# Gates of two more chunks spread by TensorE, one store of all gates, clearing divided among engines, and unread matmuls at the start

## The chip, the cores and the metric

One core of a Trainium2 chip runs the whole program: TensorE (PE), VectorE (DVE), ScalarE (ACT), GpSimd (POOL) and SyncE (SP), which issues nearly all DMAs here. Each engine works off its own list of instructions in order; between engines, semaphores order the work. The metric is the device time of one launch in microseconds. The kernel before takes 523.4 us, the median of three runs (523.13 to 523.64).

## The reference

Three layers follow each other: an mLSTM attention over 2 sequences of 768 steps with 8 heads of width 40, a mixture of 8 experts with the two best per token, and a dense layer with x cos(x) in its middle. Only the first one matters for the change:

```python
for t in range(S):
    m_new = np.maximum(f_gate[:, :, t] + m, i_gate[:, :, t])
    f_stab = np.exp(f_gate[:, :, t] + m - m_new)
    i_stab = np.exp(i_gate[:, :, t] - m_new)
    m = m_new
    C = f_stab * C + i_stab * np.einsum('bhd,bhe->bhde', vt, kt)
    n = f_stab * n + i_stab * kt
    h_tilde = np.einsum('bhde,bhe->bhd', C, qt)
    y[:, :, t] = sigmoid(o_gate) * h_tilde / max(abs(n . qt), 1)
```

## The kernel before, in words

The steps of time are cut into 6 chunks of 128 for each of 2 sequences, 12 chunk steps in all. Within a chunk the recurrence becomes matmuls: scores of queries and keys (`mm_s`, line 247), weights made of the gates (`mk_w`, line 209, and a triangular select on POOL, line 210), their product (`mk_p`, line 256), the output from the product and from the state of the chunk before (`mm_out`, lines 306 and 310), and the new state (`mm_state`, line 266; `mk_state`; `mk_decay`).

The gates lie with the 16 pairs of sequence and head on partitions and time along the free axis. `gates_a` runs the recurrences for a range of chunks on DVE (lines 90 to 97: a scan, two elementwise operations, a clamp, a running sum for each chunk); `gates_b` (lines 108 to 110) makes two further rows from them; `gates_t` transposes the gates on TensorE (line 121), and `gates_c` copies the results to `tok`, `tokG` and `kdec`. The weights need the running sum of a head along time on all 128 partitions. There are two ways to this. For chunks 0 and 1, `mm_g` (line 196) spreads it by TensorE, eight transposes of a column of `tokG` into two PSUM banks, from which ScalarE reads. For all others, `gates_a` stores the sums to DRAM (`GD`, line 102), and `load_gb` (line 175) reads them back with the partition axis repeated, 512 KB for each chunk. There are two stores: chunks 0 to 3, and chunks 4 and 5. `mk_w` and `mk_e` (lines 223 and 226) read either the PSUM banks (`pg`) or the loaded tile (`gb`).

The order of each engine's list is the order of the calls in the program. Ahead of the loop, lines 808 to 837 call the loads, the gates of chunks 0 to 3, and the scores, weights and product of chunks 0 and 1. In the loop, step n (`att_step`) makes the output of chunk n, the scores and weights of chunk n + 2 and the product of chunk n + 1, and issues loads ahead (`loads`). SP's list holds these loads, the stores of the gates and those of the outputs, in order. PSUM tiles come from rotating pools: `psA` of four banks, `psS` of three, `psM` of one. A new tile waits until all readers of the tile that had its bank are done. `psS` serves `mm_g`, `mm_state` and `mm_out`; `psM` serves the transposes of the gates and of the outputs (`rt_a`, `rt_b`).

Clearing: the tiles for queries and keys have unused rows that have to be zero, as have those for `kb` and the state. POOL clears them (lines 137, 141, 145), DVE half of one (line 136).

Of the kernel before, what the change touches and what calls it, by code (L numbers as in the profile page):

```python
# [9 lines left out]
FT = mybir.dt.float32  # L10
FR = mybir.dt.float32r
BF = mybir.dt.bfloat16
I32 = mybir.dt.int32
U32 = mybir.dt.uint32
AF = mybir.ActivationFunctionType
# [3 lines left out]
B, H, S, D = 2, 8, 768, 40  # L19
NH = H // 2  # L20
C = 128
# [19 lines left out]
def tile_mlstm_moe_moe2(ctx, tc, qk, kv, og, gi, gf, wcat, noise, wm1, wm2, cst, out):  # L41
# [15 lines left out]
    def psS():  # L57
        return ps.tile([128, 512], FT, name="pS", tag="S", bufs=3)

    def psM():  # L60
        return ps.tile([128, 512], FT, name="pM", tag="M", bufs=1)
# [7 lines left out]
    ident = cp.tile([128, 128], FT, name="ident")  # L69
    cc_ = cp.tile([128, 341], FT, name="cc")  # L70
    A.preload_act_table_set("exp_and_others")

    g_r = cp.tile([16, C], FT, name="g_r")
    V.memset(g_r, 1.0)
    V.memset(g_r[:, 0:1], 0.0)
    V.memset(g_s, 0.0)
    tok = cp.tile([128, NC, 16], FT, name="tok")
    tokG = cp.tile([128, 2, 16], FT, name="tokG")
    kdec = cp.tile([128, NC, 16], FT, name="kdec")
    GD = dr.tile([NC, 16, C], FT, name="gd")  # L80

# [2 lines left out]
    def gates_a(c0, c1):  # L84
        a, z = c0 * C, c1 * C
        s = slice(a, z)
        a1 = max(a, 1)
        if a == 0:
            V.memset(g_g[:, 0:1], 0.0)
        V.tensor_tensor_scan(out=g_m[:, s], data0=g_f[:, s], data1=g_i[:, s],  # L90
                             initial=(-1e30 if a == 0 else g_m[:, a - 1:a]), op0=OP.add, op1=OP.max)
        V.tensor_tensor(out=g_g[:, a1:z], in0=g_f[:, a1:z], in1=g_m[:, a1 - 1:z - 1], op=OP.add)
        V.tensor_tensor(out=g_g[:, a1:z], in0=g_g[:, a1:z], in1=g_m[:, a1:z], op=OP.subtract)
        V.tensor_scalar(g_g[:, a1:z], g_g[:, a1:z], -110.0, None, op0=OP.max)
        for c in range(c0, c1):
            V.tensor_tensor_scan(out=g_G[:, c * C:(c + 1) * C], data0=g_r, data1=g_g[:, c * C:(c + 1) * C],
                                 initial=0.0, op0=OP.mult, op1=OP.add)
        if c0 < 2:
            A.activation(gG[:, s], g_G[:, s], AF.Copy)
        if c0 >= 2:  # L100
            d0 = 0 if c0 == 2 else c0
            Y.dma_start(GD[d0:c1].rearrange("c p t -> p c t"),
                        g_G[:, d0 * C:c1 * C].rearrange("p (c t) -> p c t", t=C))

    def gates_b(c0, c1):
        n = c1 - c0
# [16 lines left out]
    def gates_c(c0, c1):  # L123
        pv = PT[c0]
        V.tensor_copy(tok[:, c0:c1, :], pv[:, :, 0:16])
        if c0 < 2:
            V.tensor_copy(tokG[:, c0:c1, :], pv[:, :, 64:80])
        A.activation(kdec[:, c0:c1, :], pv[:, :, 32:48], AF.Exp)


    NB = 3
    QKS, KBS, STS = [], [], []
    for i in range(NB):
        t = ap_.tile([128, 4, NH, C], FT, name=f"qk{i}")
        if i == 1:
            V.memset(t[:, 0:2], 0.0)
        G.memset(t[:, 2 * (i == 1):], 0.0)
        QKS.append(t)
    for i in range(2):
        t = ap_.tile([128, H, 64], FT, name=f"kb{i}")  # L140
        G.memset(t, 0.0)
        KBS.append(t)
    for i in range(2):
        t = ap_.tile([128, NH, 82], FT, name=f"st{i}")
        G.memset(t, 0.0)
        STS.append(t)
    XD = dr.tile([B * S, KW], FT, name="xd")
    KO = H * D
# [12 lines left out]
    def load_qk(n):  # L161
        if n >= 2 * NC:
            return
        b, c = divmod(n, NC)
        d = L[n]
        t = d["qk"] = QKS[n % NB]
        Y.dma_start(t[0:D, 0:3], qk[b, c, 0])
        Y.dma_start(t[64:64 + D, 1:4], qk[b, c, 1])

    def load_gb(n):  # L170
        if n >= 2 * NC:
            return
        b, c = divmod(n, NC)
        t = L[n]["gb"] = ap_.tile([128, H, C], FT, name="gb", bufs=3)
        Y.dma_start(t, bass.AP(tensor=GD.tensor, offset=GD.offset + (c * 16 + b * H) * C,
                               ap=[[0, 128], [C, H], [1, C]]))
# [11 lines left out]
    def mm_g(n):  # L188
        b, c = divmod(n, NC)
        d = L[n]  # L190
        d["pg"] = []
        for u in range(2):
            p = psS()
            for w in range(4):
                h = b * H + 4 * u + w
                T.transpose(p[:, 128 * w:128 * w + 128], tokG[:, c, h:h + 1].to_broadcast([128, 128]), ident)
            d["pg"].append(p.rearrange("p (h t) -> p h t", t=C))

    def mk_w(n):
        if n >= 2 * NC:  # L200
            return
        b, c = divmod(n, NC)
        d = L[n]
        pg = [d["gb"][:, 0:4], d["gb"][:, 4:8]] if n >= 2 else d["pg"]
        w = d["w"] = ap_.tile([128, H, C], FT, name="wt", bufs=2)
        for u in range(2):
            for k in range(4):
                h = 4 * u + k
                A.activation(w[:, h, :], pg[u][:, k, :], AF.Exp, bias=tok[:, c, b * H + h:b * H + h + 1])
            G.affine_select(out=w[:, 4 * u:4 * u + 4, :], in_=w[:, 4 * u:4 * u + 4, :], pattern=[[0, 4], [1, C]],  # L210
                            compare_op=OP.is_ge, fill=0.0, base=0, channel_multiplier=-1)

    def mk_e(n):
        if n >= 2 * NC:
            return
        b, c = divmod(n, NC)
        d = L[n]
        if c:
            e = d["ge"] = ap_.tile([128, NH, C], FT, name="get", bufs=2)
            for s in range(2):  # L220
                r = slice(64 * s, 64 * s + 64)
                if n >= 2:
                    A.activation(e[r], d["gb"][r, s:H:2, :], AF.Exp)
                else:
                    for u in range(2):
                        A.activation(e[r, 2 * u:2 * u + 2, :], d["pg"][u][r, s:4:2, :], AF.Exp)
        if c < NC - 1:
            kb = d["kb"] = KBS[n % 2]
            G.tensor_tensor(out=kb[:, :, 0:D], in0=d["k"],
                            in1=kdec[:, c, b * H:b * H + H][:, :, None].to_broadcast([128, H, D]), op=OP.mult)  # L230
# [127 lines left out]


    tri = cp.tile([128, 128], BF, name="tri")  # L360
    ones = cp.tile([128, 128], BF, name="ones")
    io128 = cc_[:, 128:256]
    io32 = cc_[:, 256:288]
    tid = cc_[:, 288:300]
# [4 lines left out]
    def late_consts():  # L369
        Y.dma_start(cc_, cst[:, 128:469])  # L370
        Y.dma_start(wc, wcat)
        Y.dma_start(nz, noise)
# [433 lines left out]


    Y.dma_start(ident, cst[:, 0:128])
    load_qk(0)
    load_kv(0)  # L810
    load_qk(1)
# [11 lines left out]
    gates_b(1, 2)  # L823
    gates_t(1, 2)
    mm_s(0, (2, 3))
    gates_a(2, 4)
    gates_c(1, 2)
    mk_e(0)
    late_consts()
    load_gb(2)  # L830
    mk_p(0)
    mm_g(1)
    mk_w(1)
    mm_s(1)
# [3 lines left out]

    def loads(n):
        load_qk(n + 3)  # L840
        if n > 2 or n == 0:
            load_gb(n + 3)
        load_kv(n + 2)
        if n < 5:
            load_o(n + 1)
        if n == 2:
            load_gb(4)
            load_gb(5)

    def att_step(n):  # L850
        if n == 0:
            loads(0)
        if n:
            mk_e(n + 1)
        for f, a in pre.pop(n, []):
            f(*a)
        mm_state(n)
        if n:
            mm_s(n + 2, (0,))
        mm_out(n, (lambda w: mm_s(n + 2, (w + 1,))) if n else None)  # L860
        if n == 0:
            gates_t(2, 4)
        if n:
            rt_a(n - 1, psS if n == 7 else None)
        mm_s(n + 2, (3,) if n else range(NH))
        for f, a in mid.pop(n, []):
            f(*a)
        if n:
            rt_b(n - 1, psS if n == 9 else None)
        if n == 2:  # L870
            gates_t(4, NC)
        mk_state(n)
        mk_p(n + 1)
        mk_q(n + 1)
        mk_decay(n + 1)
        if n == 0:
            gates_c(2, 4)
        if n == 2:
            gates_c(4, NC)
        if n == 1:  # L880
            gates_a(4, NC)
        loads(n + 1)
        if n == 2 * NC - 1:
            mk_y(n)
        for f, a in fill.pop(n, []):
            f(*a)
        if n < 2 * NC - 1:
            mk_y(n)
        mk_w(n + 2)
        if n == 0:  # L890
            V.tensor_copy(tri, cc_[:, 0:128])
            V.tensor_copy(rb[:, 0], row0)
            V.memset(ones, 1.0)
            V.memset(os_[:, NC], 0.0)
        if n == 1:
            gates_b(4, NC)
        if n == 10:

            for p, r0, st, m in ((64, ROW0[2] + CAP2, 512, 6), (16, CAP1, 256, 2), (16, ROW1[0] + CAP1, 256, 2)):
                Y.dma_start(bass.AP(tensor=YD.tensor, offset=YD.offset + r0 * DM, ap=[[DM, p], [st * DM, m], [1, DM]]),  # L900
                            cc_[:p, None, 0:DM].to_broadcast([p, m, DM]))
# [128 lines left out]
    with tc.If(over > 0):  # L1030
        WD = [dr.tile([S, E], FT, name=f"wd{b}") for b in range(B)]
        for b in range(B):
            r = R[b]
# [125 lines left out]
```

## Time and profile before

| | |
|---|---|
| three timed runs | 523.64, 523.13, 523.40 us |
| profiled execution, its own time | 525.03 us |
| its span, first to last instruction | 523.3 us |
| PE busy | 490.2 us (94%) |
| DVE, ACT, POOL busy | 372.1, 325.7, 278.5 us |
| mean granted clock of TensorE | 0.992 |

Busy shares are means over the whole span. The attention steps are the first fifth of it; behind them the experts and the dense layer follow. A line of a timeline has the start, the time (of all instructions merged into it), engine, line, operation, what it writes and reads, and in brackets how long the engine was idle before it and what ended that. `x8` means eight instructions; a TensorE call on 32-bit data makes two or more of them. An engine's time on a line is not its occupation alone: neighbouring instructions overlap at their ends.

### The profile page before, as it was taken

What the parts mean: (1) busy time and instruction counts of PE and PEld (TensorE: products, weight loads), DVE (VectorE), ACT (ScalarE), POOL (GpSimd) and SP (SyncE); (2) the same over time, 40 slices, a digit from 0 to 9 for tenths busy, and PEclk for the clock granted to TensorE, in tenths of its full rate; (3) what the DMA queues carried; (4) which work ended last, traced back from release to release, by engine and by line L of the source; (5) the groups of instructions that cost most, each with busy time, mean ns of one, the idle gap of its engine ahead of it and who ended that gap; (6) DMA issues with size and microseconds to landing.
All of it is one profiled execution on the core that took longest, in us unless ns stands there. A gap on an engine that the chain in (4) does not pass through costs nothing.

```text
span 523.3 us, 9036 instructions
## 1 busy us (share of the span) xinstructions
PE 490.2 (94%) x3198; PEld 468.1 (89%) x3198; DVE 372.1 (71%) x791; ACT 325.7 (62%) x695; POOL 278.5 (53%) x246
## 2 busy tenths in 40 slices
PE   4799998999999999999999987999999999999994
PEld 3688887999899999999999976899999999999994
DVE  8774497678378777777775689688856665787772
ACT  3647867466465454545454655578787777777772
POOL 6445468665846867685857696274365347300000
PEclk9999999899999999999999999999999999999998
DMA  6789894695563828291929193030021003001001
GB/s 182 209 281 266 279 278 155 188 363 172 216 248 117 313 88 330 69 372 44 380 88 319 42 360 105 29 115 14 0 76 39 1 8 95 13 2 39 1 1 44
DMA packets 25909, 77.69 MB, mean 148 GB/s; under 512 B 3872, under 2 KB 11552, under 8 KB 25856
## 3 DMA queue, kind: packets, MB, share of 16 engines
q1 hardware_dynamic: 22752, 67.50, 37.2%
q0 software_dynamic: 3104, 9.54, 6.1%
q8 instruction: 27, 0.44, 0.3%
q14 instruction: 26, 0.21, 0.1%
HBM read 67.41 MB, written 9.62 MB: 147 GB/s over the span
## 4 chain that ended last, share of the span: by engine, by line
PE 69%; DVE 14%; DMA 7%; issue 4%; ACT 3%; POOL 2%; SPq 0%; DVEq 0%; POOLq 0%; ACTq 0%
PE pS L589 31%; PE pA L598 9%; PE pA L595 9%; PE pA L594 9%; DMA gb<-gd 2%; DMA xgt<-xd,idx 2%; PE pM L551 2%; PE pS L310 2%; PE pA L247 1%; PE pM L351 1%; PE pA L607 1%; PE pA L606 1%; POOL wl L582 1%; DVE xt L674 1%; DVE c_t L713 1%
## 5 line engine op out<-in xcount | busy, mean ns | idle before, releaser
L582 POOL TENSOR_TENSOR wl<-wraw,wh 128x704 fp32r<-128x704 f32 x69 | 122.9, 1787 | 59.9 <-ACT wh L580 56.3
L644 DVE SCALAR_TENSOR_TENSOR hb<-pS,hb 128x384 fp32r<-128x384 f32 (+2 forms) x128 | 45.9, 390 | 46.4 <-ACT hb L641 45.8
L580 ACT ACTIVATE wh<-wraw 128x704 fp32r<-128x704 f32 x80 | 62.8, 785 | 14.6 <-PE pA L606 8.2
L589 PE MATMUL pS<-xh,wh 128*128 128x448 f32 (+1 forms) x240 | 69.5, 344 | 0.4 <-ACT xh L553 0.4
L589 PE MATMUL pS<-xh,wl 128*128 128x448 f32 (+1 forms) x240 | 66.3, 330 | 0.9 <-POOL wl L582 0.9
L589 PE MATMUL pS<-xh,w 128*128 128x384 f32 x288 | 66.4, 339 | 0.5 <-DVE m_t L754 0.5
L594 PE MATMUL pA<-wh,hb 128*128 128x320 f32 x208 | 62.2, 309 | 0.0
L595 PE MATMUL pA<-wl,hb 128*128 128x320 f32 x208 | 62.2, 309 | 0.0
L739 ACT ACTIVATE m_t<-pS,magic 128x384 f32<-128x384 f32 x64 | 37.1, 579 | 30.4 <-PE pS L589 29.3
L641 ACT ACTIVATE hb<-pS 128x448 fp32r<-128x448 f32 (+1 forms) x80 | 37.6, 471 | 26.9 <-PE pS L589 20.0
L589 PEld LDWEIGHTS pS<-xh,w 128*128 128x128 f32 x288 | 50.0, 188 | 1.2 <-DVE m_t L754 1.1
L598 PE MATMUL pA<-wh,hb 128*128 128x320 f32 x208 | 44.3, 313 | 4.0 <-DVE hb L644 4.0
L754 DVE SCALAR_TENSOR_TENSOR m_t<-m_t,pS 128x384 f32<-128x384 f32 x64 | 35.4, 553 | 15.4 <-ACT m_t L753 15.1
L589 PEld LDWEIGHTS pS<-xh,wl 128*128 128x128 f32 x240 | 43.1, 190 | 3.3 <-POOL wl L582 1.1
L740 DVE TENSOR_SCALAR m_t<-m_t 128x384 f32<-128x384 f32 x64 | 23.3, 365 | 28.8 <-ACT m_t L739 28.6
L589 PEld LDWEIGHTS pS<-xh,wh 128*128 128x128 f32 x240 | 40.9, 190 | 1.4 <-ACT xh L553 0.6
L760 POOL TENSOR_TENSOR wl<-m_t,wh 128x384 fp32r<-128x384 f32 x25 | 25.4, 1017 | 31.0 <-ACT wh L758 21.7
L589 PE MATMUL pS<-xl,wh 128*128 128x448 f32 (+1 forms) x160 | 39.6, 329 | 0.0
L594 PEld LDWEIGHTS pA<-wh,hb 128*128 128x128 f32 x208 | 38.6, 186 | 0.6
L595 PEld LDWEIGHTS pA<-wl,hb 128*128 128x128 f32 x208 | 38.7, 186 | 0.6
L598 PEld LDWEIGHTS pA<-wh,hb 128*128 128x128 f32 x208 | 33.0, 186 | 6.0 <-DVE hb L644 5.9
L542 POOL DMA_INDIRECT xgt<-xd,idx x28 | 34.0, 1215 | 7.8 <-issue 3.4
(203 smaller groups left out, 1251.0 us busy)
## 6 DMA issues: line engine op xcount, KB each, us to landing
wraw<-wm SPq DMA_DIRECT2D x36, 704.0 KB
raw<-wm SPq DMA_DIRECT2D x16, 704.0 KB
qk<-qk SPq DMA_DIRECT2D x24, 240.0 KB
gb<-gd SPq DMA_DIRECT2D x10, 512.0 KB
kv<-kv SPq DMA_DIRECT2D x12, 324.0 KB
yd<-yt SPq DMA_DIRECT2D x22, 160.0 KB
wraw<-wm SPq DMA_DIRECT2D x8, 352.0 KB
xd<-xt SPq DMA_DIRECT2D x12, 192.0 KB
```

The source lines that it names most:

```text
L542: G.indirect_dma_start(out=t[:n, :], out_offset=None, in_=XD[0:S, :] if g < 2 else XD[:, :], in_offset=bass.IndirectOffsetOnAxis(ap=(idxe ...
L580: A.activation(wh, raw[:, f, :], AF.Copy)
L582: eng.tensor_tensor(out=wl, in0=raw[:, f, :], in1=wh.bitcast(FT), op=OP.subtract)
L589: T.matmul(p[:, :n], w[:, 128 * k:128 * k + 128], x[:, m, :], start=(i == 0), stop=(i == 7))
L594: T.matmul(a[:n, :DM], hh[:, s], wh[:, KW:], start=first, stop=False)
L595: T.matmul(a[:n, :DM], hh[:, s], wl[:, KW:], start=False, stop=False)
L598: T.matmul(a[:n, :DM], hl[:, s], wh[:, KW:], start=False, stop=last)
L641: A.activation(hh[:, :n], p[:, :n], AF.Relu)
L644: V.scalar_tensor_tensor(out=hb[:, o:o + z - a], in0=p[:, a:z], scalar=0.0, in1=hh[:, a:z].bitcast(FT), op0=OP.max, op1=OP.subtract)
L739: A.activation(t, m["p"], AF.Identity, bias=magic, scale=0.5 / PI)
L754: V.scalar_tensor_tensor(out=s, in0=s, scalar=1.0, in1=m["p"], op0=OP.subtract, op1=OP.mult)
L760: eng.tensor_tensor(out=m["hl"], in0=m["t"], in1=m["hh"].bitcast(FT), op=OP.subtract)
```

## The change

- `tokG` holds four chunks instead of two, and `gates_a` copies the sums of chunks 2 and 3 to the tile that is transposed (ScalarE, line 99), as it did for chunks 0 and 1. The chunks 2 and 3 are spread by `mm_g`, called in steps 0 and 1 for chunk n + 2, after the output's normalization is issued; the second half goes to the bank of `psM`. Their exponentials (`mk_g`, taken out of `mk_e`) follow their weights.
- The first store is gone, and so are the loads of chunks 2 and 3. One store of all six chunks is issued with `gates_a(4, 6)` in step 1.
- Ahead of the loop, `mk_p(0)` moves in front of `gates_a(2, 4)`, and both move behind `gates_c(1, 2)` and `mk_e(0)`.
- Clearing: POOL clears the first tile for queries and keys and half of the second; ScalarE clears the rest by copies of a zero column; DVE clears `kb` and the state tiles.
- The bf16 tile of ones is set at the start, and 14 matmuls of 128x384 on it are issued into a `psM` tile that nobody reads.

```diff
+    ones = cp.tile([128, 128], BF, name="ones")
+    V.memset(ones, 1.0)
...
-    tokG = cp.tile([128, 2, 16], FT, name="tokG")
+    tokG = cp.tile([128, 4, 16], FT, name="tokG")
...
-        if c0 < 2:
+        if c0 < 4:
             A.activation(gG[:, s], g_G[:, s], AF.Copy)
-        if c0 >= 2:
-            d0 = 0 if c0 == 2 else c0
-            Y.dma_start(GD[d0:c1].rearrange("c p t -> p c t"),
-                        g_G[:, d0 * C:c1 * C].rearrange("p (c t) -> p c t", t=C))
+        else:
+            Y.dma_start(GD.rearrange("c p t -> p c t"), g_G.rearrange("p (c t) -> p c t", t=C))
...
-        if c0 < 2:
+        if c0 < 4:
             V.tensor_copy(tokG[:, c0:c1, :], pv[:, :, 64:80])
...
+    zero = cp.tile([128, 1], FT, name="zero")
+    V.memset(zero, 0.0)
     for i in range(NB):
         t = ap_.tile([128, 4, NH, C], FT, name=f"qk{i}")
-        if i == 1:
-            V.memset(t[:, 0:2], 0.0)
-        G.memset(t[:, 2 * (i == 1):], 0.0)
+        if i == 0:
+            G.memset(t, 0.0)
+        else:
+            if i == 1:
+                G.memset(t[:, 0:2], 0.0)
+            for k in range(2 * (i == 1), 4, 2):
+                v = t[:, k:k + 2].rearrange("p a w t -> p (a w t)")
+                A.activation(v, zero.to_broadcast([128, 2 * NH * C]), AF.Copy)
...
-            p = psS()
+            p = psM() if u and n > 1 else psS()
...
+    def mk_g(n):
+        d = L[n]
+        e = d["ge"] = ap_.tile([128, NH, C], FT, name="get", bufs=2)
+        for s in range(2):
+            r = slice(64 * s, 64 * s + 64)
+            if n >= 4:
+                A.activation(e[r], d["gb"][r, s:H:2, :], AF.Exp)
+            else:
+                for u in range(2):
+                    A.activation(e[r, 2 * u:2 * u + 2, :], d["pg"][u][r, s:4:2, :], AF.Exp)
...
+    junk = psM()
+    for i in range(14):
+        T.matmul(junk[:, 0:384], ones, ones[:, None, :].to_broadcast([128, 3, 128]), start=True, stop=True)
...
     mm_s(0, (2, 3))
-    gates_a(2, 4)
     gates_c(1, 2)
     mk_e(0)
+    mk_p(0)
+    gates_a(2, 4)
     late_consts()
-    load_gb(2)
-    mk_p(0)
     mm_g(1)
     mk_w(1)
...
-        if n > 2 or n == 0:
+        if n > 2:
             load_gb(n + 3)
...
             mk_y(n)
+        if n < 2:
+            mm_g(n + 2)
         mk_w(n + 2)
+        if n < 2:
+            mk_g(n + 2)
```

## Rows read from the trace of the kernel before

**Rows 1.** Table by stretch: us, busy time of each engine, granted clock, DMA

```profile
135.00:320.00 185.00, 180.17 (x1111) 172.31 (x1110) 135.43 (x224) 98.84 (x175) 133.06 (x85) 1.00 0.59 218
```

**Rows 2.** Chain of waits, 0 to 62 us: start, us, what

```profile
29.41 4.29 DMA gd<-g_all
33.76 5.75 DMA gb<-gd
```

**Rows 3.** Timeline of ScalarE, 0 to 50 us

```profile
6.27 0.31 ACT L99 ACTIVATE g_all<-g_all 16x128 f32<-16x128 f32 x1 [4.17 <-DVE g_all L96]
...
9.02 2.17 ACT L209 ACTIVATE wt<-pS,tok 128x128 f32<-128x128 f32 x8 [0.93 <-PE pS L196]
...
15.00 2.17 ACT L209 ACTIVATE wt<-pS,tok 128x128 f32<-128x128 f32 x8 [0.47 <-PE pS L196]
17.01 1.32 ACT L226 ACTIVATE get<-pS 64x256 f32<-64x256 f32 x4
...
21.65 2.45 ACT L209 ACTIVATE wt<-gb,tok 128x128 f32<-128x128 f32 x8 [0.86 <-DMA gb<-gd]
...
39.60 2.44 ACT L209 ACTIVATE wt<-gb,tok 128x128 f32<-128x128 f32 x8 [1.05 <-DMA gb<-gd]
```

**Rows 4.** Timeline of TensorE, 7 to 71 us

```profile
11.77 1.99 PE L247 MATMUL pA<-qk 128*128 128x256 f32 x4
14.31 1.09 PE L196 MATMUL pS<-ident,tokG 128*128 128x128 f32 x8 [0.55 <-DVE tokG L127]
15.23 1.89 PE L247 MATMUL pA<-qk 128*128 128x256 f32 x8
...
18.11 2.01 PE L310 MATMUL pS<-kv,ppt 128*128 128x82 f32 x16 [0.27 <-ACT get L226]
...
21.87 0.88 PE L266 MATMUL pS<-kv,kb 128*104 128x82 f32 x8
24.76 0.67 PE L247 MATMUL pA<-qk 128*128 128x256 f32 x2 [2.02 <-DMA qk<-qk]
...
44.40 0.94 PE L351 MATMUL pM<-wc,xTt 128*128 128x128 f32 x6 [0.91 <-ACT xTt L344]
...
70.95 0.29 PE L440 MATMUL pM<-r_os,ones 128*128 128x48 bf16 x6
```

**Rows 5.** Timeline of SP's DMA issues, 14 to 18 us

```profile
14.13 0.34 SPq L102 DMA_DIRECT2D gd<-g_all  x1
...
17.78 0.32 SPq L167 DMA_DIRECT2D qk<-qk  x1
```

**Rows 6.** Timeline of DVE, 2 to 27 us

```profile
2.15 0.91 DVE L136 MEMSET qk<- 128x1024 f32 x1 [0.16 <-issue]
...
3.28 0.41 DVE L90 TENSOR_TENSOR_SCAN g_all<-g_all 16x128 f32<-16x128 f32 x1 [0.20 <-DMA g_all<-gi]
...
4.36 1.44 DVE L94 TENSOR_SCALAR g_all<-g_all 16x127 f32<-16x127 f32 x1
...
8.85 0.21 DVE L94 TENSOR_SCALAR g_all<-g_all 16x128 f32<-16x128 f32 x1
...
10.36 1.05 DVE L90 TENSOR_TENSOR_SCAN g_all<-g_all 16x256 f32<-16x256 f32 x1
...
13.38 0.73 DVE L96 TENSOR_TENSOR_SCAN g_all<-g_r,g_all 16x128 f32<-16x128 f32 x2
...
26.04 0.73 DVE L90 TENSOR_TENSOR_SCAN g_all<-g_all 16x256 f32<-16x256 f32 x1
```

**Rows 7.** Timeline of POOL, 5 us

```profile
5.20 1.06 POOL L141 MEMSET kb<- 128x512 f32 x2
```

**Rows 8.** Table by stretch around the first gather, columns as in rows 1

```profile
91.00:92.00 1.00, 0.55 (x3) 0.31 (x3) 0.00 (x0) 0.72 (x2) 1.00 (x3) 1.00 0.82 267
90.00:95.00 5.00, 3.53 (x17) 3.10 (x18) 1.94 (x6) 1.89 (x5) 4.55 (x6) 0.72 0.78 222
95.00:100.00 5.00, 5.00 (x42) 5.00 (x42) 4.80 (x13) 1.89 (x5) 2.88 (x3) 0.94 0.29 110
```

More of the change, by code (lines that the diff above doesn't have):

```diff
@@ L140, in tile_mlstm_moe_moe2 @@
         t = ap_.tile([128, H, 64], FT, name=f"kb{i}")
-        G.memset(t, 0.0)
+        V.memset(t, 0.0)
         KBS.append(t)
@@ L144, in tile_mlstm_moe_moe2 @@
         t = ap_.tile([128, NH, 82], FT, name=f"st{i}")
-        G.memset(t, 0.0)
+        V.memset(t, 0.0)
         STS.append(t)
@@ L203, in mk_w @@
         d = L[n]
-        pg = [d["gb"][:, 0:4], d["gb"][:, 4:8]] if n >= 2 else d["pg"]
+        pg = [d["gb"][:, 0:4], d["gb"][:, 4:8]] if n >= 4 else d["pg"]
         w = d["w"] = ap_.tile([128, H, C], FT, name="wt", bufs=2)
@@ L217, in mk_e @@
         d = L[n]
[L218 to L226, printed above, removed]
+        if c and n not in (2, 3):
+            mk_g(n)
         if c < NC - 1:
@@ L360, in tile_mlstm_moe_moe2 @@
     tri = cp.tile([128, 128], BF, name="tri")
-    ones = cp.tile([128, 128], BF, name="ones")
     io128 = cc_[:, 128:256]
@@ L892, in att_step @@
             V.tensor_copy(rb[:, 0], row0)
-            V.memset(ones, 1.0)
             V.memset(os_[:, NC], 0.0)
```

## The prediction

> **What bounds the kernel now.** I read the page's busy shares first, then a table by stretch, then the chain of waits, then the timelines of the single engines in the first 45 us. From 135 us on TensorE works 180.2 of 185 us [rows 1], so whatever the start gains or loses is still there at the end unless a wait takes it up on the way. All that the change touches lies before 45 us, and there TensorE does wait. The chain of waits [rows 2] runs, for the second chunk step, through the store of the gates of chunks 4 and 5 (29.41 us, 4.29 us until it has landed) and the load that reads it back, spread over all partitions (33.76, 5.75 us). ScalarE's weights of chunk 4 wait 1.05 us for that load and begin at 39.60 [rows 3], and TensorE waits 0.91 us at 44.40 for ScalarE work queued behind them [rows 4]. The other large hole is 2.02 us before 24.76 [rows 4], when the scores of chunk 3 wait for their queries and keys. That load goes out only at 17.78 [rows 5], because the spread load of chunk 2, ahead of it on SP, waits for the first store (14.13). Before that DVE sets the pace (the gate recurrences), and TensorE is at its lower level, 1.2 GHz: four score matmuls take 1.99 us at 11.77, eight take 1.89 us at 15.23 [rows 4], though the granted-clock column says 1.00 there too.
>
> **The change, part by part.** The sum is made on the profiled execution, span 523.3 us in a run of 525.03; the three timed runs have a median of 523.40, and I put the difference onto that.
>
> *Clearing.* DVE loses a 1024-wide clear of 0.91 us and gets two 512-wide and two 328-wide ones, the ones and a zero column: at 0.91/1024 about 0.46 x 2 + 0.3 x 2 + 0.2 + 0.06 = 1.8 us, 0.9 more. It had 0.20 us of idle time before the first scan [rows 6], so the scan at 3.28 begins about 0.7 late. Against that, the clamp at line 94 took 1.44 us at 4.36 while POOL was clearing (its kb clears begin at 5.20 [rows 7]) and 0.21 us for the next chunk at 8.85 [rows 6]. With POOL done by about 3.5 it should take 0.21. Net -0.5 us (bounds -1.2 if the added clears cost nothing, +0.7 if the clamp stays slow). ScalarE's three 1024-wide copies fit into the 4.17 us of idle time before 6.27 [rows 3]: 0.31 us for 128 wide and 2.17/8 = 0.27 us each in a row bound one at 0.31 to 2.5 us, and 1.1 to 1.3 (between them, by length) ends them near 6, where the cover ends too: 0 to 0.2 us late.
>
> *Unread matmuls.* Nothing waits for their result, and TensorE has no work before 6.6. Six 48-wide bf16 matmuls took 0.29 us at 70.95 [rows 4], of which most is the tail of one; 0.02 to 0.05 us each makes 0.16 to 0.4 us for 384 columns, 2.3 to 5.6 us for 14, twice that at the lower level only for the first of them. I take 4.5 us, ending near 5.7: they hide. What they may bring is the upper clock for the first gates and scores: four spreads take 0.55 instead of about 1.1 us, so ScalarE's first weights, at 9.02 before, begin at 9.02 - 0.5 - 0.5 = 8.0, and the second half of the first scores takes 0.95 instead of 1.99.
>
> *The new order of chunks 0 to 2.* Weights 8.0 to 10.2, gate copy of chunk 1 to 10.5 [rows 3], transposes and the second half of the scores to 11.75, the product of chunk 0 (line 256) on DVE to 12.45: two microseconds earlier than before. But it now stands ahead of the recurrences of chunks 2 and 3, which took 10.36 to 14.11 [rows 6]. Without POOL beside them (the same scan took 0.73 us at 26.04, not 1.05) they take 2.6 to 3.75; I take 2.75, so to 15.2. And here the change adds a wait. Chunks 2 and 3 now have a copy on ScalarE (line 99, 256 wide, 0.31 to 0.62, say 0.42), issued ahead of the weights of chunk 1. Queued behind it are those eight weights and the four gate exponentials. They begin at 15.7, before at 15.00 [rows 3]: +0.7 us. For those exponentials TensorE waits: the output of chunk 0 takes the PSUM bank that they read, as the 0.27 us before 18.11 shows [rows 4]. So that output moves from 18.11 to 18.8.
>
> *Spreading by TensorE.* The spread of chunk 2 comes behind the output of chunk 0 and the scores of chunk 2: 18.11 to 21.87 was 3.76 us [rows 4], so 22.55. It takes 1.09 us (14.31, the same eight), so the state of chunk 1 moves to 23.65. The hole of 2.02 us goes: on SP nothing holds the load of chunk 3 back but the scores of chunk 0, so it goes out near 12, not at 17.78. The scores of chunk 3 begin at 24.5 against 24.76. The spread of chunk 3 stands in a full step, so +1.09: TensorE is 0.85 us late from 30 us on.
>
> *One store.* Chunk 2's weights, 21.65 before [rows 3], begin one half spread after 22.55, at 23.25: +1.6. From PSUM they take 2.17 instead of 2.45 us, the exponentials 1.32 as at 17.01 instead of two longer ones of about the same sum; so DVE reaches the recurrences of chunks 4 and 5 at 27.35 instead of 26.04 and ends them 0.8 to 1.35 us later. The store then carries 48 KB instead of 16. The queues are emptier, as two loads of 512 KB are gone; the first store landed within 3.65 us (14.13 to 17.78 [rows 5]), the second in 4.29 [rows 2]. With 3.2 to 4.3 and then 5.75 again the weights of chunk 4 could begin at 39.0 to 40.9. TensorE's own lateness lets them begin at 39.60 - 1.05 + 0.85 = 39.4 at best. Between 39.4 and 40.9 I take 40.2: +0.6 us, and what would then be late is the transposed output behind them (44.40), as now. So the sum without more is 523.4 + 0.6 = 524.0.
>
> *The clock.* TensorE, faster at first, has done the spread and scores of chunk 1 (1.09 and 1.89 us) and its state work (0.88) by 15.5, and then has nothing until 18.8: a gap of 3.3 us. The trace has two nearby cases [rows 8]. After 2.02 us of nothing at 22.74 the clock held. Behind the stretch before 92, in which TensorE did little but transposes (0.55 us busy from 91 to 92, still at 1.00), the granted clock was 0.72 over 90 to 95 us and 0.94 over 95 to 100: 2.8 and 0.6 us, together 3.4 us at 1.2 GHz. The gap here is emptier than that stretch and longer than the one that held. If the clock falls, some 3.4 us of the output of chunk 0, the scores and the spread of chunk 2 run at half the rate: 1.7 us later, all of it on the way both to the store and to TensorE's next steps. That makes 525.7. The Trainium skill, TensorE: Matmul & The Clock Gate, section "Why this matters for your kernels", speaks against the change here: it asks to leave no long idle gaps between bursts, since one puts the array back to half its rate. By that rule the sum is 525.7, by the row that held 524.0; the stretch at 92 agrees with the rule.
>
> **The rivals.** *The clock holds* over the gap: 524.0, worked out above. For it: the 2.02 us that did no harm; against: the longer gap. *The unread matmuls leave the clock low*: they end near 5.7, then come a pause and transposes; if TensorE is at 1.2 GHz until 13.8 as now, the weights of chunk 0 begin 0.5 and the scores end another 1.0 later; the recurrences, ScalarE's copy and the weights of chunk 1 follow, and the gap shrinks: 524.0 + 1.5 = 525.5. *Not slower*: the half-rate stretch of 3.4 us behind 92 goes. It stands behind the gather at which TensorE idles; with other transfer times in front of it, or the steps shifted, the clock may hold there. That gives back up to 1.7 us, so 524.0 - 1.7 = 522.3. It decides from the point where the granted clock in the step after the first gather stays at 1.00. Against it: nothing that the change does touches that gather's own wait. *The change doesn't do what it says*, by the order on ScalarE, is in the forecast already; if the added clears cost nothing and the recurrences take 2.6, the copy comes at its old time and the case is 523.2, which I count with the clock that holds.
>
> **How the numbers follow.** Forecast, the clock falls: 0.42, 525.7. The clock holds: 0.24, 523.2 to 524.8. The start stays at the low clock: 0.15, 525.5. Not slower: 0.19, 521.6 to 523.4. A difference below 0.2%, 1.05 us, can't be told from none in this kernel. Slower by more: 0.38 + 0.06 + 0.12 = 0.56. Within: 0.04 + 0.16 + 0.03 + 0.07 = 0.30. Faster: the rest of the last case and a little of the second, 0.14. The range for 8 in 10 reaches from inside the last case, 522.1, to 527.0, the forecast with the recurrences at 3.75 and the store at 4.3.
>
> **What would show it.** The clamp at line 94 at 0.2 us near 5.2; the first score matmuls at 0.24 us each; a copy of 16x256 on ScalarE that ends near 15.6 with the weights of chunk 1 right behind it; TensorE idle for about 3 us until the output of chunk 0 near 18.8, released by ScalarE; score matmuls of chunk 2 at 0.48 us each where the clock fell, 0.24 where it held; no wait for queries and keys near 24; the store leaving at 30 to 32.5 and the weights of chunk 4 beginning at 40 to 42. The prediction is wrong if the weights of chunk 1 begin before 15.0, or if the output of chunk 0 doesn't wait for ScalarE, or if the steps after 45 us catch up what the start lost.

## The result, and the profile after

The changed kernel takes 528.05 us (median of six runs, 527.47 to 529.05), the kernel before beside it 523.52 (522.86 to 525.26): a ratio of 1.0084 [1.0062, 1.0107], so 4.5 us slower. The forecast was 2.3 us slower, 525.7, and its range ended at 527.0. The sign and the mechanism came as forecast; the size did not.

The head of the profile after, and its granted clock in 40 slices:

```profile
span 526.5 us, 9097 instructions
PE 497.4 (94%) x3228; PEld 473.1 (90%) x3228; DVE 370.5 (70%) x796; ACT 328.6 (62%) x703; POOL 275.4 (52%) x241
...
PEclk8799999899999999999999999999999999999998
```

TensorE is busy 7.2 us longer than before; 3.8 of them are the unread matmuls. The first two slices of the clock say where to look for the rest. The table by stretch of the changed kernel (us, busy time of PE, PEld, DVE, ACT, POOL, granted clock, DMA share, GB/s):

```profile
5.00:10.00 5.00, 2.98 (x12) 2.68 (x13) 3.87 (x15) 2.28 (x10) 0.46 (x1) 0.74 0.98 259
10.00:15.00 5.00, 4.96 (x29) 3.87 (x29) 3.53 (x9) 0.99 (x4) 1.56 (x3) 0.92 0.75 236
15.00:20.00 5.00, 1.33 (x9) 1.17 (x8) 3.67 (x9) 4.42 (x14) 2.44 (x4) 0.77 0.70 223
20.00:25.00 5.00, 5.00 (x23) 4.65 (x22) 1.43 (x6) 0.31 (x3) 1.63 (x3) 0.55 0.52 138
...
18.00:19.00 1.00, 0.00 (x0) 0.00 (x0) 0.67 (x2) 0.99 (x5) 0.80 (x2) 0.50 0.63 245
24.00:25.00 1.00, 1.00 (x5) 0.83 (x5) 0.93 (x3) 0.00 (x0) 0.00 (x0) 0.76 1.01 230
...
95.00:100.00 5.00, 4.68 (x27) 4.68 (x28) 4.18 (x12) 2.68 (x8) 4.17 (x3) 0.66 0.70 230
...
135.00:320.00 185.00, 181.14 (x1113) 172.73 (x1111) 134.81 (x226) 98.44 (x174) 133.27 (x84) 1.00 0.58 213
```

A slice of 5 us at 0.77 holds 2.3 us at 1.2 GHz, one at 0.55 holds 4.5: together 6.8 us, from 17.7 to 24.5 (the expectations below say 6.9). From 135 us on it is as in [rows 1]. What fills those microseconds stands in TensorE's timeline of the changed kernel:

```profile
1.14 3.84 PE L822 MATMUL pM<-ones 128*128 128x384 bf16 x14 [1.14 <-DVE ones L73]
...
7.28 1.87 PE L203 MATMUL pS<-ident,tokG 128*128 128x128 f32 x8 [0.35 <-DVE tokG L127]
8.94 1.91 PE L258 MATMUL pA<-qk 128*128 128x256 f32 x4
...
14.52 0.88 PE L277 MATMUL pS<-kv,kb 128*104 128x82 f32 x8
19.07 3.71 PE L321 MATMUL pS<-kv,ppt 128*128 128x82 f32 x16 [3.67 <-ACT get L229]
...
22.84 2.75 PE L258 MATMUL pA<-qk 128*128 128x256 f32 x8
25.42 0.60 PE L203 MATMUL pS<-ident,tokG 128*128 128x128 f32 x4
...
27.01 0.64 PE L258 MATMUL pA<-qk 128*128 128x256 f32 x2
...
47.39 0.94 PE L362 MATMUL pM<-wc,xTt 128*128 128x128 f32 x6 [0.72 <-ACT xTt L355]
```

The line at 19.07 is the case in one row. TensorE had nothing for 3.67 us, ScalarE's gate exponentials let it go, and the 16 matmuls that took 2.01 us in [rows 4] took 3.71. The eight scores at 22.84 took 2.75 instead of 1.89. The 2.02 us hole at 24.76 in [rows 4] is gone: the scores of chunk 3 at 27.01 wait for nothing. The work behind the weights of chunk 4 (`pM<-wc,xTt`), at 44.40 before, stands at 47.39 now. ScalarE's timeline of the changed kernel gives the cause of the gap:

```profile
8.33 2.17 ACT L216 ACTIVATE wt<-pS,tok 128x128 f32<-128x128 f32 x8 [0.82 <-PE pS L203]
...
15.53 0.41 ACT L101 ACTIVATE g_all<-g_all 16x256 f32<-16x256 f32 x1 [3.79 <-DVE g_all L98]
15.96 2.17 ACT L216 ACTIVATE wt<-pS,tok 128x128 f32<-128x128 f32 x8
17.97 1.32 ACT L229 ACTIVATE get<-pS 64x256 f32<-64x256 f32 x4
...
42.59 2.45 ACT L216 ACTIVATE wt<-gb,tok 128x128 f32<-128x128 f32 x8 [0.86 <-DMA gb<-gd]
```

ScalarE idled 3.79 us for the recurrences of chunks 2 and 3, copied them for gate transposes that come seven microseconds later (22.57), and only then made the weights and exponentials of chunk 1, behind which POOL's select, DVE's product and TensorE's output of chunk 0 all stand. The other end of the path, the store and the load behind it, in the timeline of SP's issues and the chain of waits of the changed kernel:

```profile
33.29 0.33 SPq L103 DMA_DIRECT2D gd<-g_all  x1
...
35.42 0.86 SPq L182 DMA_DIRECT2D gb<-gd  x2
```

```profile
35.42 7.08 DMA gb<-gd
42.59 2.45 ACT wt L216 x8
```

### The profile page after: what moved, and what is told of

Its sections match the earlier page's. It is cut to its first block, busy times and chain, and to the rows that moved or that the text cites. A ratio compares the mean times of both kernels' runs of the same rounds, so it can differ in the third digit from the quotient of the medians.

```text
span 526.5 us, 9097 instructions
## 1 busy us (share of the span) xinstructions
PE 497.4 (94%) x3228; PEld 473.1 (90%) x3228; DVE 370.5 (70%) x796; ACT 328.6 (62%) x703; POOL 275.4 (52%) x241
## 4 chain that ended last, share of the span: by engine, by line
PE 74%; DVE 12%; ACT 5%; DMA 3%; issue 3%; POOL 0%; SPq 0%; DVEq 0%; POOLq 0%; ACTq 0%
PE pS L599 33%; PE pA L608 9%; PE pA L605 9%; PE pA L604 9%; PE pS L321 2%; PE pA L258 2%; PE pM L561 2%; DMA gb<-gd 1%; ACT wt L216 1%; PE pM L362 1%; PE pA L617 1%; PE pA L616 1%; DMA xgt<-xd,idx 1%; DVE hb L654 1%; DVE xt L684 1%
## 5 line engine op out<-in xcount | busy, mean ns | idle before, releaser
L651 ACT ACTIVATE hb<-pS 128x448 fp32r<-128x448 f32 (+1 forms) x80 | 37.7, 471 | 27.0 <-PE pS L599 20.1
```

The costliest lines, as they stand in the source:

```text
L651: A.activation(hh[:, :n], p[:, :n], AF.Relu)
```

## The experiments

The lines of the changed kernel that are shown here stand up to eleven behind those of before. Ratios are to the kernel before, run on the same chip; its median beside the experiments lay between 523.8 and 524.4.

**1. The gap filled** (e1_fill). The changed kernel, with 20 more unread bf16 matmuls between the state of chunk 0 and the output of chunk 0.

```diff
         mm_state(n)
+        if n == 0:
+            f = psM()
+            for i in range(20):
+                T.matmul(f[:, 0:384], ones, ones[:, None, :].to_broadcast([128, 3, 128]), start=True, stop=True)
```

> The changed kernel with 20 more unread bf16 matmuls of 128x384 between the state matmuls of chunk 0 and its output, where TensorE has nothing for 3.67 us (15.4 to 19.07). Nothing else differs. Theory (the clock): at 2.4 GHz they take some 3.2 us and fit the gap; the clock then holds from 17.7 to 24.5 us, score matmuls of chunk 2 take 0.24 instead of 0.48 us, and half of 6.9 us, 3.4 us, comes back: about 524.6. Rival (the order: late weights of chunk 1 and two added spreads of 1 us each): the clock's stretch is hidden by other waits, the time stays within 0.5 us of 528.0. Third: 2.0 us or less comes back, because the load of the gates, not TensorE, then sets the weights of chunk 4.

524.19 us, ratio 0.9998 [0.998, 1.0016]. Its TensorE timeline:

```profile
19.17 2.01 PE L321 MATMUL pS<-kv,ppt 128*128 128x82 f32 x16 [0.42 <-ACT get L229]
21.16 1.93 PE L258 MATMUL pA<-qk 128*128 128x256 f32 x8
22.93 0.60 PE L203 MATMUL pS<-ident,tokG 128*128 128x128 f32 x4
```

Its table by stretch:

```profile
15.00:20.00 5.00, 4.58 (x33) 3.02 (x32) 3.78 (x9) 4.32 (x14) 2.34 (x4) 1.00 0.66 215
20.00:25.00 5.00, 5.00 (x40) 4.69 (x40) 2.08 (x10) 1.79 (x9) 2.13 (x5) 1.00 0.57 155
```

The output of chunk 0 starts no earlier (19.17), since it waits for ScalarE all the same. But the granted clock is 1.00 from 17 to 26 us, the output takes 2.01 again, and the spread of chunk 2 stands 2.5 us earlier than in the changed kernel; the weights of chunk 4 3.0 earlier (39.62) and the span 3.8 shorter. So the lateness of ScalarE alone cost next to nothing; what the clock lost in the gap cost 3.9 us of the median (4.1 us, if each median is taken against that of the kernel before beside it). The last 0.8 us of the span come behind 45 us: at 130.45 the changed kernel waits 0.40 us for the data of a gather, where this one does not wait, and the distance between the two traces grows from 2.8 to 3.3 us there and to 3.7 later.

**2. The copy issued later** (e2_latecopy). The changed kernel, the ScalarE copy of the sums of chunks 2 and 3 put behind the weights and exponentials of chunk 1.

```diff
-        if c0 < 4:
+        if c0 < 2:
             A.activation(gG[:, s], g_G[:, s], AF.Copy)
-        else:
+        elif c0 >= 4:
...
     mk_e(1)
+    A.activation(gG[:, 2 * C:4 * C], g_G[:, 2 * C:4 * C], AF.Copy)
```

> The changed kernel with ScalarE's copy of the gate sums of chunks 2 and 3 issued behind the weights and exponentials of chunk 1, not ahead of them. Nothing else differs. Theory (the wait on ScalarE opens the gap, the gap lets the clock fall): the weights of chunk 1 begin near 12.6 instead of 15.96, the output of chunk 0 near 15.8 instead of 19.07, TensorE's gap shrinks below 1 us, the clock holds, the spread of chunk 2 begins near 19.5 instead of 25.4: 5 to 6 us less, 522 to 523. Rival (two spreads on TensorE and the clearing are what costs): 1 us or less comes back, 527 or more.

524.38 us, 1.001 [0.9992, 1.0029]. Its TensorE timeline, and its chain of waits:

```profile
15.31 2.01 PE L321 MATMUL pS<-kv,ppt 128*128 128x82 f32 x16 [0.27 <-ACT get L229]
18.66 0.33 PE L121 MATMUL pM<-ident,g_all 80*128 80x80 f32 x2 [1.33 <-DVE g_all L110]
...
42.98 0.94 PE L362 MATMUL pM<-wc,xTt 128*128 128x128 f32 x6 [0.87 <-ACT xTt L355]
```

```profile
30.85 7.24 DMA gb<-gd
```

The queue order is the cause of the gap: one copy moved, and the output of chunk 0 stands at 15.31, 3.8 us earlier, and the clock holds. I had expected more than 3.7 us back. The rest went to a new wait of 1.33 us for the recurrences and to the load of the gates, which took 7.24 us; the weights of chunk 4 wait for it as before, at 38.18.

**3. No unread matmuls** (e3_nojunk). The changed kernel without the 14 matmuls at the start.

> The changed kernel without the 14 unread matmuls at the start. Theory (they raise the clock too early and it has fallen again by 7.4 us, so they bring little; the gap before the output of chunk 0 stays): first scores at 1.2 GHz, weights of chunk 1 up to 1 us later, the fall of the clock stays: 527.5 to 529. Rival (they shift the clock's rise and fall so that it falls in the gap): without them the clock rises near 13.8 as before the change and holds over the shorter gap: 525 or less.

527.57 us, 1.0069 [1.0047, 1.009], inside what the theory allowed. The changed kernel without them has the same gap and a shorter stretch at half rate; its table by stretch and its TensorE timeline:

```profile
20.00:23.00 3.00, 3.00 (x16) 2.82 (x15) 0.37 (x3) 0.37 (x3) 1.68 (x3) 0.52 0.31 81
23.00:26.00 3.00, 3.00 (x22) 2.73 (x21) 1.50 (x7) 0.77 (x4) 0.23 (x1) 0.91 0.99 256
```

```profile
19.12 2.81 PE L321 MATMUL pS<-kv,ppt 128*128 128x82 f32 x16 [3.67 <-ACT get L229]
```

Here the stretch is 3.4 us, 20.1 to 23.5, what I had forecast for the change. So one gap can be followed by different lengths at half rate. Here the clock even held through the gap and fell at 20.1, one microsecond after work had begun again. The spans of the two traces differ by 1.0 us, the medians by 0.5; as the runs of the two kernels scatter over 526.38 to 528.71 and 527.47 to 529.05 us, 0.5 and 1.0 can't be told apart. This trace has another stretch at half rate at 315 to 325 us, which the traces of the changed kernel have not. It holds the time up by little: it takes 1.4 us, but at 323.16 the changed kernel waits 0.94 us where this one does not wait, and behind that 0.3 us are left of it.

**4. The kernel before once more** (e0_before) and **5. before with the divided clearing alone** (e4_clear).

> The kernel before once more, for a second trace. The profiled execution was 525.03 us, 1.6 us above the median of the three runs shown. If the half-rate stretch behind 92 us (3.4 us long) is what the slower executions of it have and the others not, this trace has either a span near 521.8 without the stretch or one near 523.3 with it; if the stretch is always there, it is here too with a span near 521.8, and the 1.6 us lies elsewhere.

> The kernel before with the divided clearing alone (ScalarE and DVE take parts of POOL's clears). Theory (a term of the sum, -0.5 us): the clamp at line 94 takes 0.2 instead of 1.44 us, the first scan begins 0.6 us later, the transposes of chunk 0 begin 0.5 us earlier, and all behind them moves along: 523.2 if before is 523.7. Rival: the loads of queries, keys and gates set the later steps, nothing moves behind 20 us: 523.7.

Before took 524.74 us, span 523.0, with the half-rate stretch behind 90 us there again (0.70 and 0.95; 0.72 and 0.94 in [rows 8]). The third trace (experiment 12) has it too, with a span of 521.2, so it is not what sets these executions apart. The divided clearing alone took 524.24, 0.9992 [0.9971, 1.0013]. Its DVE and its TensorE timeline:

```profile
4.79 0.21 DVE L94 TENSOR_SCALAR g_all<-g_all 16x127 f32<-16x127 f32 x1
```

```profile
6.36 0.36 PE L121 MATMUL pM<-ident,g_all 80*128 80x80 f32 x1 [6.36 <-DVE g_all L110]
...
24.65 0.67 PE L254 MATMUL pA<-qk 128*128 128x256 f32 x2 [2.69 <-DMA qk<-qk]
```

The clamp is short and the transposes come 0.8 us earlier, but nearly all of it is lost in the wait for the queries of chunk 3, which grew from 2.02 to 2.69 us: these scores begin at 24.65, at 24.76 in [rows 4] (and at 23.97 and 23.75 in the other two traces of before). In this trace the clock was at half rate from 26 to 29 us, behind that wait. The interval is too wide to show or to exclude the 0.5 us.

**6. The old order of chunks 0 to 2** (e5_oldorder). The changed kernel, with the three calls ahead of the loop in the order of before.

```diff
     mm_s(0, (2, 3))
+    gates_a(2, 4)
     gates_c(1, 2)
     mk_e(0)
-    mk_p(0)
-    gates_a(2, 4)
     late_consts()
+    mk_p(0)
```

> The changed kernel with the old place of the recurrences of chunks 2 and 3: ahead of the gate copies of chunk 1 and of the product of chunk 0, as before the change. ScalarE's copy of their sums stays ahead of the weights of chunk 1. Nothing else differs. Theory (the new order opens the gap in which the clock falls): DVE ends the recurrences near 13.5 us, weights of chunk 1 near 14.4 instead of 15.96, output of chunk 0 near 17.5 instead of 19.07 with less than 0.5 us of idle time before it, as TensorE's spread and scores of chunk 1 come later; the clock holds, spread of chunk 2 near 21.4 instead of 25.4: 523.5 to 524.5. Rival (the copy on ScalarE opens it, in any order): a gap of 2 us or more stays, the clock falls, 526 or more.

524.97 us, 1.0008 [0.9986, 1.003]. The output of chunk 0 waits 0.27 us and starts at 17.48, and the clock holds from 15 to 25 us. The gap is a matter of this order, then; the time is half a microsecond above the range that I had expected, on a chip where the kernel before had a median of 524.43.

**7 and 8. A better version** (e6_best, e7_best_nojunk). The copy late as in 2; the scores of chunk 2 ahead of the transposes of the gates of chunks 2 and 3; the store behind the other loads of step 1, just ahead of the load that reads it. The second also leaves out the unread matmuls.

```diff
...
         if n == 0:
+            mm_s(2)
             gates_t(2, 4)
...
         if n == 2:
+            Y.dma_start(GD.rearrange("c p t -> p c t"), g_G.rearrange("p (c t) -> p c t", t=C))
             load_gb(4)
```

> The changed kernel with three edits: the copy of the gate sums of chunks 2 and 3 behind the weights and exponentials of chunk 1; the scores of chunk 2 ahead of the transposes of the gates of chunks 2 and 3 on TensorE; the store of all gates behind the loads for chunks 4 and 5 (queries and keys, keys and values, output gates), just ahead of the loads that read it. Theory: with the copy alone late the time was 524.4, with 1.33 us of idle time before those transposes and 1.02 us of ScalarE's wait for the load of the gates of chunk 4, while the DMA engines stood still from 26 to 30 us. The first edit of the two new ones gives about 1 us, the second starts 1.1 MB of loads up to 2.5 us sooner and so takes ScalarE's wait away, 0.9 us: 522.5, below before. Rival: the gates' load and the two spreads on TensorE keep the time where it was, 524.

> The same with the three edits, without the 14 unread matmuls. Theory (they raise the clock from the first scores on in some executions only, and nothing on the path of the time waits for the first scores): the same time as with them, within 0.5 us. Rival: the first scores and spreads at 1.2 GHz delay the product of chunk 0, the recurrences and all behind them by 1 to 1.5 us.

523.39 us, 0.9983 [0.9965, 1.0], with the unread matmuls, and 522.58, 0.9973 [0.9955, 0.9991], without: the second beats both kernels, if by little. I had expected 522.5 of the first, and of the second the same time within 0.5 us; the 0.8 us between their medians is not clear of the scatter of 12 runs each (522.18 to 524.24, 521.96 to 524.50). The TensorE timeline of the second:

```profile
7.22 1.97 PE L201 MATMUL pS<-ident,tokG 128*128 128x128 f32 x8 [0.35 <-DVE tokG L125]
...
16.56 2.01 PE L319 MATMUL pS<-kv,ppt 128*128 128x82 f32 x16 [0.27 <-ACT get L227]
22.04 0.65 PE L201 MATMUL pS<-ident,tokG 128*128 128x128 f32 x4 [1.55 <-DVE tokG L125]
...
43.54 0.94 PE L360 MATMUL pM<-wc,xTt 128*128 128x128 f32 x6 [0.21 <-ACT xTt L353]
```

At 43.54 TensorE waits 0.21 us for the work behind the weights of chunk 4, where it waited 0.91 in [rows 4]. What is left is 1.55 us ahead of the spread of chunk 2.

**9 and 10. The changed kernel twice more** (e8_again, e9_again), to see whether the length of the stretch changes from run to run.

> The changed kernel once more, for a second trace. What is open is the size of the half-rate stretch: 6.9 us in the changed kernel's first trace (17.7 to 24.5), 3.4 us in the one without the unread matmuls, with the same gap of 3.67 us. Theory A (its length varies from execution to execution between one such stretch and two): here 3.4 or 6.9, and the spread of chunk 2 begins near 24.5 or 25.4. Theory B (with the unread matmuls it is always 6.9): 6.9 again.

> The changed kernel a third time, for the same question: 3.4 us of half rate or 6.9, and whether there is an execution in which the clock holds over the gap (then the span is near 523).

528.45 and 527.68 us. The TensorE timeline of the one, then of the other:

```profile
19.01 3.71 PE L321 MATMUL pS<-kv,ppt 128*128 128x82 f32 x16 [3.67 <-ACT get L229]
25.52 0.60 PE L203 MATMUL pS<-ident,tokG 128*128 128x128 f32 x4
```

```profile
19.16 3.71 PE L321 MATMUL pS<-kv,ppt 128*128 128x82 f32 x16 [3.67 <-ACT get L229]
25.41 0.60 PE L203 MATMUL pS<-ident,tokG 128*128 128x128 f32 x4
```

Three traces of three have the long stretch: the granted clock over 15 to 20 and 20 to 25 us is 0.79 and 0.53 in the one, 0.75 and 0.56 in the other, which makes 6.8 and 6.9 us. All three of these executions have a mean granted clock of 0.984; the other five timed runs of the changed kernel lie between 0.986 and 0.991, so the traces don't show that every execution has it.

**11. The hole of before closed by itself** (e10_earlyload). The kernel before, the load of the queries of chunk 3 issued ahead of the spread load of chunk 2.

```diff
+    load_qk(3)
     late_consts()
     load_gb(2)
...
-        load_qk(n + 3)
+        if n:
+            load_qk(n + 3)
```

> The kernel before with one edit: the load of queries and keys of chunk 3 goes out on SP behind the first store of the gates, ahead of the constants and of the spread load of chunk 2, so that the 2.0 us hole of TensorE at 22.7 should close. Theory (the chain through the second store and the load of the gates of chunks 4 and 5 sets the weights of chunk 4, and DVE reaches it no sooner): the hole goes, the time stays within 0.5 us. Rival (TensorE's hole is what counts, and the change's gain of 2 us there is real): 1.5 to 2 us less.

524.66 us, 1.0017 [0.9992, 1.0042]. TensorE is busy for all of 20 to 25 us; the hole is gone. Its ScalarE and its TensorE timeline, and its table by stretch:

```profile
38.62 2.45 ACT L209 ACTIVATE wt<-gb,tok 128x128 f32<-128x128 f32 x8 [2.38 <-DMA gb<-gd]
```

```profile
43.42 0.94 PE L351 MATMUL pM<-wc,xTt 128*128 128x128 f32 x6 [2.24 <-ACT xTt L344]
```

```profile
45.00:50.00 5.00, 5.00 (x28) 4.61 (x27) 3.00 (x7) 3.89 (x11) 2.65 (x5) 0.69 0.88 249
```

Closing the hole brought nothing in the end. The scores of chunk 3 begin 2.2 us earlier than in [rows 4] (22.57). Of this 1.2 us are gone at 43.42 (44.40 in [rows 4]): the time passes through the store and the load of the gates, and the waits there grew by 1.33 us each, to 2.38 and 2.24. Behind the longer wait the clock fell, 0.69 over 45 to 50 us, and this took the other microsecond and 0.7 us more. So in this trace the clock took more than the chain did, and what the closed hole is worth where the clock holds is not shown. In the changed kernel the same hole went; that it gained as little there is argued, not measured.

**12. The kernel before a third time** (e11_before2).

> The kernel before, unchanged, profiled once more. In the first trace of it the store of the gates took 4.29 us and the weights of chunk 4 began at 39.60; in the second 2.15 us and 38.25, with one new wait of 0.84 us at 51.41 behind it; both executions lie over 1 us above the kernel's median. Theory: the slow store of the first trace is the exception, so the store takes about 2.1 us here, the weights of chunk 4 begin at 38.0 to 38.6 and, without a wait like that at 51.41, the execution takes 523.0 to 523.8 us. Rival: the store takes anything between 2 and 4.3 us and what it gives is taken back later in any case; then the time is 524 to 525.5 whatever the store takes.

522.89 us, span 521.2. Its chain of waits, and its ScalarE timeline:

```profile
28.92 2.97 DMA gd<-g_all
31.95 4.61 DMA gb<-gd
```

```profile
37.70 2.45 ACT L209 ACTIVATE wt<-gb,tok 128x128 f32<-128x128 f32 x8 [0.25 <-DMA gb<-gd]
```

Store and load together took 7.58 us here, 8.96 in the second trace (2.15 and 6.81) and 10.04 in the first [rows 2]. The weights of chunk 4 begin at 37.70, 38.25 and 39.60, and the executions take 522.89, 524.74 and 525.03 us. My theory named the store; in these three it is store and load together, and in the second trace a wait of 0.84 us at 51.41 took most of it back. Three traces don't say what makes one execution of this kernel longer than another in general. The 35 timed beside experiments 5 to 8 run from 522.22 to 526.76 us, and there the time goes with the mean granted clock: the 12 with a clock up to 0.990 have a median of 525.75 us, the 9 from 0.994 on one of 522.95. Where their half-rate stretches lie is not known.

## Why the prediction failed

*Clearing* came as worked out: clamp 0.22 us, transposes of the gates at 6.67 instead of 7.15, so −0.48. By itself it brought nothing that could be measured (experiment 5).

*Unread matmuls*: 3.84 us for 14, hidden, ended at 4.98 (4.5, near 5.7). The upper clock that they bring did not last: the granted clock is 0.74 over 5 to 10 us, the first spreads take 1.87 us, little less than the 1.97 without them (experiment 8), and the first four scores 1.91. The weights of chunk 0 began at 8.33, not 8.0, and product 0 was done at 12.8, not at 12.45. It is not so in every execution: in the TensorE timeline of experiment 2, with the same start, the spreads ran at the upper clock, as I had forecast.

```profile
1.14 4.66 PE L822 MATMUL pM<-ones 128*128 128x384 bf16 x14 [1.14 <-DVE ones L73]
...
7.28 1.09 PE L203 MATMUL pS<-ident,tokG 128*128 128x128 f32 x8 [0.35 <-DVE tokG L127]
```

*The new order* was right in every link. Recurrences of chunks 2 and 3 from 12.79 to 15.50 (12.45 to 15.2), the copy on ScalarE behind them, weights of chunk 1 at 15.96 (15.7), the output of chunk 0 held by the gate exponentials to 19.07 (18.8). Experiments 2 and 6 show both causes apart: either the late copy or the old order closes the gap.

*Spreading* was right: no wait for the queries of chunk 3, and one spread more in each of two steps. A transpose is one instruction here, so `x4` is half a spread and the two halves stand in two lines; from 25.42 to the state behind them at 26.30 they take 0.88 us, where I had 1.09.

*The clock* is the step that failed, by its size: the 1.7 us that I added for it. That it would fall over this gap was right, and experiment 1 shows that the fall, not the wait, is what costs. But I took 3.4 us at 1.2 GHz from the one stretch of [rows 8] and all of it as work. It was 6.8 us, beginning inside the gap; 5.4 of it lay on the output and scores of chunk 2, which lost 1.70 and 0.86 us: 2.6 where I had 1.7. With the 0.27 us that the output was later anyway, the spread of chunk 2 came at 25.42 instead of 22.55 + 1.7 = 24.25. Nor did the price stay what it was there: with the clock held in experiment 1, 2.5 us come back at this spread, 3.8 in the span and 3.9 in the median, against the 1.7 of the forecast.

One stretch in one trace was no bound for the next: after the same gap without the unread matmuls it was 3.4 us (experiment 3), with them 6.8 to 6.9 in three traces. The Trainium skill, TensorE: Matmul & The Clock Gate, section "Why this matters for your kernels", asks to leave no long idle gap between bursts of matmuls; the traces agree, with 1.2 GHz behind the gap of 3.67 us in all four traces that had it empty, and a granted clock of 1.00 from 17 to 25 us where it was filled or closed (experiments 1, 2, 6). That section gives no time for one gap; mine came from [rows 8], and there the forecast went wrong.

*One store*: it landed in 2.1 us, less than the 3.2 to 4.3 that I had allowed, and the load took 7.08 us, more than 5.75; nearly the same sum. DVE's recurrences before it began at 30.24 against 27.35 + 1.7, 1.2 us late (0.9 by the clock, 0.27 by the later output); with 0.5 of that back, the weights of chunk 4 came at 42.59 against 40.2 + 1.7 = 41.9. But the row I measured from was at fault too. At 39.60 [rows 3] stands a slow passage through store and load; other executions of before begin those weights 1.35 and 1.9 us earlier. So the traces that I compared differ by 3.2 us in span, and the medians by 4.5: the first trace of before lies 1.5 us above its median, that of the changed kernel 0.2 above. I had put the difference onto the median as if this surplus were the same in both. So of the 2.35 us that the forecast was short, 0.9 stand between the two traces (3.2 us of span, 2.3 forecast), 1.3 come from where the two traces lie among the runs of their kernels, and 0.1 from the median of before, 523.52 instead of 523.40.

*Not slower* fell: the half-rate stretch behind the first gather stayed (0.66 over 95 to 100 us). It can be absent: in the trace of experiment 6 the clock is 1.00 from 90 to 100 us, and its span is 521.1 us. *The clock holds* fell for the changed kernel; experiment 1, which makes it hold, measures 524.19, where that rival had 524.0. *The clock left low at the start* is half true, as the spreads and the first scores show, but the gap did not shrink for it.

One thing stays open: why the half-rate stretch is 6.8 us behind one gap and 3.4 behind the same gap without the matmuls at the start.

## What to carry to other kernels

Before a copy is put into an engine's list ahead of its need, look at what it waits for and at what stands behind it: here a copy that nobody wanted for seven microseconds held up three other engines. A gap on TensorE costs not only itself but what its clock loses behind it, and where the chain has slack the gap may be free and the clock is the whole price; twenty unread matmuls inside the gap bought it back, while fourteen at the start of the kernel bought nothing that could be measured. And closing a hole gains only if the chain passes through it: look at what waits next, and whether the clock holds over that wait. Take the row that carries a sum from more than one trace, and look at the granted clock of each run beside its time.

## What the runs showed of the hardware

- Half rate began inside the idle time, at about 17.7 us, and outlasted it by 5.4 us of solid matmuls; in experiment 3 it began only at 20.1, behind the end of the same gap. Other waits of TensorE were followed by half rate as well: 2.69 us in experiment 5 (0.66 over 25 to 30), 2.24 in experiment 11 (0.69 over 45 to 50); 2.02 us in [rows 4] was not. The stretch behind 90 us in [rows 8] follows waits of 0.92, 0.25 and 0.62 us among transposes; in experiment 6 waits of 0.92, 0.24 and 0.60 us stand at the same place, and the clock held.
- The same load of 512 KB of gates took 4.61 to 7.24 us where the chain of waits shows it, and the store ahead of it 2.1 to 4.29, in the kernel before alone 7.58 to 10.04 together.
- The 16-partition operations of DVE ran slower beside POOL: the clamp took 1.44 us in [rows 6] and 0.21 to 0.22 where POOL had done, and in experiment 7 two running sums took 1.53 us instead of 0.73, with POOL at work from 15.0 to 17.9 us.
